# Attention and expert kernel: another issuer for one score row, another fence between bank halves, and TensorE ordered by rules in place of a list

## The chip, the cores and the metric

The kernel runs on one core of one Trainium2 chip. The metric is the device time of one execution in microseconds. Before the change it was 452.55 us, the median of three runs (452.53 to 452.61).

## The reference

Eight sequences of 448 tokens, twelve heads of 64. The first part is attention with capped scores, the second a layer in which each sequence sends its 128 best tokens through a two-layer expert:

```python
scores = cap * np.tanh(scale * (q @ k.T) / cap)      # per batch and head, 448 x 448
attn = np.exp(scores - max); attn /= attn.sum(-1) + 1e-9
x = (attn @ v), heads side by side                   # (8, 448, 768)
s = x[b] @ w_gate                                    # one score per token
top = the 128 tokens of batch b with the highest s
out = x; out[b, top] += sigmoid(s[top]) * (relu(x[b, top] @ w1) @ w2)   # 768 -> 1024 -> 768
```

## The kernel before, in words

**Tiling.** Four heads of one batch make a "double" (class `Double`): 24 doubles, three to a batch. The 448 keys of a double are cut in three chunks of 128 and one of 64. A chunk of 128 is a *unit*: its scores ("Q", `scores_mm`, lines 505 and 515) fill the one four-bank score tile `psS`; ScalarE takes tanh of it into one of four `p` slots (line 970) and exp in place (line 977); then TensorE multiplies it with the values ("V", `values_mm`, line 528, 56 products). The 64-key chunks of two neighbouring doubles share one score tile and one `p` slot and are multiplied one by one. The next Q can start when tanh has read `psS` and a `p` slot is free; the slot is free after its V. From the fifth double on, q and k are split in a high and a low part, and scores come from twelve products of full width (line 505, array shape `WIDTH`). Values run in the shape `TALL`, the rest of the scores and the 64-key values in `QUARTER`.

**Expert work** ("F"). When three doubles of a batch are done, `select_proc` adds their score parts, writes the row of 448 scores to DRAM and reads it back into every partition (`put`, line 632; `get`, line 635), counts ranks on VectorE, picks the rows with a one-hot product (line 711), and gathers them by GpSimd (line 727). `expert_proc` transposes them (line 756), multiplies with w1, applies relu, transposes, multiplies with w2, adds and scatters (line 863). A layer is a `group` (line 783): products of 64 rows in pairs, hi times hi, hi times lo and lo times hi, 72 products for w1 and 96 for w2. In the second half of a group the two row halves change banks; ahead of the first product of that half stands a `drain` of TensorE (line 797).

**Order.** All engines' orders are written by a planner (`Sim`, `Front`) that knows a duration for every task. TensorE's comes from `SCRIPT` (lines 36 to 41): Q or V in a fixed sequence, a number in front of which so many F products are put (`scripted`, line 1101). Where the script is empty, `policy` (line 1061) uses rules: if F is at hand (`backlog`), Q first, F next, V last, until `run_ready` says that four values, or all that are left of the double, can run one after the other; then V first until the double ends. Without F at hand Q and V alternate. Outside the tail only one group may be open, and none is opened once planned F work passes the total less `RESERVE` (50 us). `EARLIER` shifts the priority of single tasks of other engines. GpSimd's queue holds the `put` and `get` of batch 0, a memset for each value tile that lands (line 492), gathers and scatters.

Of the kernel before, what the change touches and what calls it, by code (L numbers as in the profile page):

```python
# [31 lines left out]
THIN_Q, THIN_V, THIN_F = "FVQ", "QFV", "VQF"  # L32
SOON = 1000
FILL = 300

SCRIPT = ("Q Q V V Q V Q V Q V V Q V Q V Q V Q V Q V Q V Q V Q V V Q V Q V Q V Q V Q V Q V Q V Q "
# [5 lines left out]

EARLIER = {('greater', 21): 1, ('hi', 29): -3, ('high', 21): -1, ('high', 23): 3, ('low', 2): -3,
           ('low', 27): -1, ('ranks', 7): -0.4, ('relu', 3): 3, ('relu', 11): 3}

LINE, LATER, FIRST = ("POOL", 1000, 2800, "gpsimd"), ("SP", 700, 900, "sync"), 1


QUARTER, TALL, WIDTH = range(3)
SWITCH, AFTER = 110, 85  # L50
MARGIN = 150
RESERVE = 50000
MOST = 4000
# [5 lines left out]
RUN, SLACK = 4, 300  # L59

SIDE = 6
DRAIN = 100

PS, PG, PH = 1.3, 1.1, 1.2
VISIBLE = {"PE": 230, "DVE": 120, "ACT": 110, "POOL": 150, "SP": 0}
# [51 lines left out]
class Sim:  # L117
# [47 lines left out]
    def finish(self, task, e, start):  # L165
        for x in task.busy:
            self.pend[x].remove(task)
        task.eng, task.start = e, start
        task.slots = []
        for r in task.take:  # L170
            s = r.next()
            r.free.remove(s)
            task.slots.append(s)
        for s, n in zip(task.slots, task.refs):
            s.refs = n
        busy = task.busy[e]
        if e == "PE":
            if task.shape != self.shape:
                busy += AFTER
            self.shape = task.shape  # L180
        end = start + busy
        self.clock[e] = end
        if e == "SP":
            self.dma = max(self.dma, start + 1500) + task.lag
            task.t = max(start + 2600, self.dma)
            end = task.t
        else:
            task.t = end + VISIBLE[e] + task.lag
        for s in task.reads:
            s = s() if callable(s) else s  # L190
            s.t = max(s.t, task.t if e == "SP" else end + 60)
            s.refs -= 1
            if s.refs == 0:
                s.ring.free.append(s)
        task.fn(task)
        if task.waiter is not None:
            w, task.waiter = task.waiter, None
            self.step(w, task)
        self.wake()
# [50 lines left out]
def allocate(tc, K):  # L250
    cp = K.const

    def t(name, shape, dt=F32):
        return cp.tile(shape, dt, name=name)
# [2 lines left out]
    K.cap = t("capc", [P, 1])  # L257
    K.ident = t("ident", [P, P])
    K.fast = t("fast", [1, 1], I32)
    K.sq = t("sq", [1, 1])  # L260
    K.sc = t("sc", [P, 1])
    K.wts = {}
# [518 lines left out]


def group(tc, K, kind, prio, pair, parts, wts, n, width, cost):
    nc = tc.nc
    ops = [(0, wts + "h", i) for i in range(n)] + [(0, wts + "l", i) for i in range(n)]
    ops += [(1, wts + "h", i) for i in range(n)]
    last = len(ops) - 1
    slot, ends, gap = None, [], []
    order = mybir.DependencyInfo(mybir.DependencyClass.NoSync, mybir.DependencyReason.DATA)
    for m in range(2 * len(ops)):  # L790
        turn, at = divmod(m, len(ops))
        part, r, i = ops[at]

        def mm(t, m=m, turn=turn, at=at, part=part, r=r, i=i):
            bank = t.slots[0] if m == 0 else slot
            if m == last + 1:
                gap.append(nc.tensor.drain().ins)
                for end in ends if K.loose else []:
                    tc.add_manual_dep(gap[0], end, order, reason="rows change banks")
            for h in (0, 1) if m != last else (1, 0):  # L800
                g = h ^ turn
                ins = nc.tensor.matmul(bank.obj[:, g, :width],  # L802
                                       lhsT=pair.obj[part][HALF[h], i, :],
                                       rhs=K.wts[r][HALF[h], i, g * width:(g + 1) * width],
                                       start=(m == 0), stop=(m == 2 * last + 1)).ins
                if m == last:
                    ends.append(ins.name)
                elif m == last + 1 and K.loose:
                    tc.add_manual_dep(ins, gap[0].name, order, reason="rows change banks")

        t = yield Task("PE", cost + (DRAIN if m == last + 1 else 0), mm, deps=[parts[i][part]], take=[] if m else [K.banks],
                       refs=[] if m else [2], reads=[pair] if m == 2 * last + 1 else [], prio=prio,
                       kind="mm" if m else "open")
        if m == 0:
            slot = t.slots[0]
            K.open += 1
    K.open -= 1
    return slot, t


def expert_proc(tc, K, b, M, idx, gt, gate, x):
    nc = tc.nc
    sim = K.sim
    S = K.S
    xe = x.slots[0]
    prio = (1, b)
    yield [K.weights["w1"]]
    xs, parts = yield from split_tasks(tc, K, lambda: xe.obj, [x, K.weights["w1"]], K.xs, [],
                                       K.ND, (0, 3 * b + 2), "turnxe")
    xs.refs = 1  # L830
    if not K.tail:
        yield [p for pair in parts.values() for p in pair]
    bank, t = yield from group(tc, K, "w1", (1, 0 if K.tail else b), xs, parts, "w1", K.ND, K.F // 2, 234)
    relus = []
    for g in range(2):
        def relu(t, g=g):
# [5 lines left out]
            else:  # L842
                nc.scalar.activation(out, src, AF.Relu)

        t = sim.add(Task(None, {"ACT": 660, "DVE": 610}, relu, deps=[t], take=[] if g else [K.hs],
                         refs=[] if g else [1], reads=[bank], prio=1, kind="relu"))
    yield [t]
    hp, parts = yield from split_tasks(tc, K, lambda: relus[0].obj, [t], K.hp, [relus[0]],
                                       K.NF, (0, 3 * b + 2), "turnh")
    hp.refs = 1  # L850
    yield [K.weights["w2"]]
    if not K.tail:
        yield [p for pair in parts.values() for p in pair]
    HH = K.DM // 2
    bank, t = yield from group(tc, K, "w2", prio, hp, parts, "w2", K.NF, HH, 177)
    ends = [sim.add(Task("DVE", 534, lambda _, g=g: nc.vector.scalar_tensor_tensor(
        out=xe.obj[:, g * HH:(g + 1) * HH], in0=bank.obj[:, g, :HH], scalar=gt.obj,
        in1=xe.obj[:, g * HH:(g + 1) * HH], op0=ALU.mult, op1=ALU.add), deps=[t, gate],
        reads=[bank, gt], prio=1, kind="combine")) for g in range(2)]
    yield ends  # L860

    def scatter(t):
# [7 lines left out]
               kind="scatter")  # L870


class Front:
# [74 lines left out]
    def score_task(self):  # L948
        K, sim, nc = self.K, self.sim, self.tc.nc
        u = self.u  # L950
        two = self.work[u]
        shape = self.score_shape()
        reads = [x.slots[0] for D, _ in two
                 for x in (D.ready(0, K) if shape == WIDTH else (D.q, D.k))]

        def emit(t):
            for i, (D, s) in enumerate(two):
# [1 line left out]
            self.u += 1  # L959
            self.S_free = None  # L960

        task = Task("PE", 1498 if shape == QUARTER else 1230, emit, shape=shape, reads=reads,
                    kind="scores")
        task.seq = 0
        sim.pend["PE"].append(task)
# [479 lines left out]
```

## Time and profile before

| | |
|---|---|
| median of three runs | 452.55 us |
| profiled execution | 453.71 us, its span 452.0 us |
| busy share of the span | TensorE 95%, weight loads 80%, ScalarE 68%, VectorE 61%, GpSimd 5% |
| granted TensorE clock | 0.995 of full |
| chain that ended last | TensorE 87%, ScalarE 5%, issue 3%, VectorE 2%, DMA 2% |

Busy time is given by engine, in microseconds and as a share of the span; TensorE's matmuls are pipelined and their ends are modelled, so the starts of neighbouring groups say more than the busy time of one. "L528" is line 528 of the kernel. In a timeline a line holds start, duration, engine, source line, operation, tile written and tiles read, shape and count; idle time before it stands in brackets with what ended it.

### The profile page before, as it was taken

How to read it: one execution, taken by the hardware profiler on the slowest of the kernel's cores; microseconds unless marked ns; L12 is line 12 of the kernel's file. 1: busy time of each engine (PE TensorE's matmuls, PEld its weight loads, DVE VectorE, ACT ScalarE, POOL GpSimd, SP SyncE). 2: the span in 40 equal slices, each digit the busy share in tenths (PEclk: the TensorE clock that was granted, in tenths of full speed). 3: DMA queues.
4: the chain of work that ended last, by engine and by line, in shares of the span. 5: the costliest groups of instructions: out<-in, count | busy, mean ns of one | idle time of the engine just before them, and what ended most of it. 6: DMA issues, size and time to landing. Idle time of an engine off the chain costs nothing.

```text
span 452.0 us, 17987 instructions
## 1 busy us (share of the span) xinstructions
PE 431.3 (95%) x8148; PEld 361.1 (80%) x8148; DVE 275.7 (61%) x846; ACT 306.8 (68%) x194; POOL 23.3 (5%) x57
## 2 busy tenths in 40 slices
PE   8889889999999999999999999999999999999993
PEld 6655477779898889898898888889888889879793
DVE  1076778986946588367765766737747665385141
ACT  4979989976697589487778766966689599311000
POOL 2000010000001000000000000000001000000000
PEclk9999999999999999999999999999999999999997
DMA  7958395664073372282372542443172223111001
GB/s 248 374 157 278 108 289 191 186 232 120 3 246 111 81 236 53 74 276 68 90 234 78 155 160 85 138 146 108 38 247 68 77 93 106 35 35 32 39 38 42
DMA packets 34022, 60.76 MB, mean 134 GB/s; under 512 B 11088, under 2 KB 21072, under 8 KB 33936
## 3 DMA queue, kind: packets, MB, share of 16 engines
q1 hardware_dynamic: 32400, 52.73, 36.4%
q0 software_dynamic: 1392, 6.56, 4.7%
q8 instruction: 66, 1.08, 0.9%
q10 hardware_dynamic: 144, 0.23, 0.2%
q14 instruction: 20, 0.16, 0.1%
HBM read 45.33 MB, written 14.17 MB: 132 GB/s over the span
## 4 chain that ended last, share of the span: by engine, by line
PE 87%; ACT 5%; issue 3%; DVE 2%; DMA 2%; POOL 0%; POOLq 0%; DVEq 0%
PE psV L528 30%; PE psT L802 23%; PE psS L505 16%; PE psS L515 8%; PE psB L802 3%; ACT p L970 3%; PE psV L802 2%; ACT p L977 2%; PE psT L756 1%; DMA p<-out,idx 1%; PE psT L1259 1%; ACT plent L970 1%; DVE xn L560 1%; PE psT L711 1%; DMA out<-xe,idx 1%
## 5 line engine op out<-in xcount | busy, mean ns | idle before, releaser
L970 ACT ACTIVATE p<-psS,sc 128x1792 f32<-128x1792 f32 x62 | 108.8, 1755 | 58.6 <-PE psS L505 32.8
L528 PEld LDWEIGHTS psV<-v,p 128*64 128x64 f32 (+1 forms) x3864 | 104.2, 137 | 20.5 <-issue 16.4
L528 PE MATMUL psV<-v,p 128*64 128x65 f32 (+1 forms) x3864 | 111.2, 222 | 4.1 <-issue 2.3
L977 ACT ACTIVATE p<-p,capc 128x1792 f32<-128x1792 f32 x62 | 111.1, 1793 | 1.8
L559 DVE RECIPROCAL rec<-psV 128x7 f32<-128x7 f32 x48 | 9.6, 200 | 71.4 <-PE psV L528 71.3
L505 PE MATMUL psS<-qh,kh 64*128 64x448 f32 x240 | 48.1, 391 | 0.5 <-ACT plent L970 0.4
L970 ACT ACTIVATE plent<-psS,sc 128x1792 f32<-128x1792 f32 x21 | 36.8, 1753 | 16.8 <-PE psS L505 12.0
L528 PEld LDWEIGHTS psV<-v,plent 128*64 128x64 f32 (+1 forms) x1288 | 35.0, 137 | 7.7 <-issue 6.9
L977 ACT ACTIVATE plent<-plent,capc 128x1792 f32<-128x1792 f32 x21 | 37.6, 1793 | 0.6
L528 PE MATMUL psV<-v,plent 128*64 128x65 f32 (+1 forms) x1288 | 37.5, 222 | 0.4 <-DVE xt L565 0.4
L515 PE MATMUL psS<-q,k 64*64 64x448 f32 x312 | 34.4, 549 | 2.5 <-ACT p L970 1.6
L594 DVE CUSTOM_DVE_ANT_0 jk<-xn,wg 128x256 bf16<-128x256 f32 x72 | 30.3, 421 | 1.4
L560 DVE TENSOR_TENSOR xn<-psV,rec 128x384 f32<-128x384 f32 x48 | 26.8, 557 | 1.9 <-DVE rec L559 0.3
L505 PEld LDWEIGHTS psS<-qh,kh 64*128 64x128 f32 x240 | 23.3, 184 | 4.0 <-ACT plent L970 0.5
L664 DVE TENSOR_SCALAR_CACHE_REDUCE jk<-row,score 128x512 bf16<-128x512 f32 (+1 forms) x32 | 23.7, 741 | 0.8
L472 DVE CAST kh<-k 128x896 fp32r<-128x896 f32 x20 | 12.8, 638 | 16.0 <-PE psS L505 15.7
L505 PE MATMUL psS<-qh,kl 64*128 64x448 f32 x120 | 22.4, 363 | 0.0
L505 PE MATMUL psS<-qh,klent 64*128 64x448 f32 x120 | 22.4, 362 | 0.0
L505 PE MATMUL psS<-qlent,kh 64*128 64x448 f32 x120 | 22.4, 362 | 0.0
L505 PE MATMUL psS<-ql,kh 64*128 64x448 f32 x120 | 22.3, 362 | 0.0
L515 PEld LDWEIGHTS psS<-q,k 64*64 64x64 f32 x312 | 10.2, 132 | 14.3 <-issue 10.2
L802 PE MATMUL psT<-w1h,xh 64*128 64x512 f32 x144 | 20.5, 407 | 0.7
(163 smaller groups left out, 619.8 us busy)
## 6 DMA issues: line engine op xcount, KB each, us to landing
v<-in_v SPq DMA_DIRECT2D x23, 455.0 KB, 4.5
q<-in_q SPq DMA_DIRECT2D x22, 448.0 KB, 4.5
k<-in_k SPq DMA_DIRECT2D x22, 448.0 KB, 5.2
out<-xn SPq DMA_DIRECT2D x24, 384.0 KB, 3.6
stage<-in_moe_w SPq DMA_DIRECT2D x4, 512.0 KB, 8.0
stage<-in_moe_w SPq DMA_DIRECT2D x5, 384.0 KB, 4.0
row<-line SPq DMA_DIRECT2D x7, 256.0 KB, 3.3
out<-xt SPq DMA_DIRECT2D x48, 32.0 KB, 3.4
```

What stands on the lines that cost most here:

```text
L472: nc.vector.tensor_copy(t.slots[0].obj, self.at(nm))
L505: tc.nc.tensor.matmul(banks[2 * r + j][:, :K.S], lhsT=a[HALF[j], r, c * P:(c + 1) * P], rhs=b[HALF[j], r, :], start=(n == 0), stop=(n == 2))
L515: tc.nc.tensor.matmul(banks[n][HALF[half], :K.S], lhsT=k[HALF[j], r, at:at + HD], rhs=q[HALF[j], r, :], start=True, stop=True)
L528: tc.nc.tensor.matmul(D.acc.obj[HALF[g], r, i * WIDE:(i + 1) * WIDE], lhsT=p[rows, h, n * HD:(n + 1) * HD], rhs=v[rows, u, :], start=(c == ...
L559: nc.vector.reciprocal(rec, blocks[:, :, K.D])
L560: nc.vector.tensor_tensor(slots[0].obj.rearrange("p c (r j d) -> p r j c d", r=2, j=2)[:, r], blocks[:, :2 * full, :K.D].rearrange("p (j c ...
L594: nc.vector.tensor_tensor_reduce(out=K.jk[:, :x.shape[1]], in0=x, in1=g, scale=1.0, scalar=0.0, op0=ALU.mult, op1=ALU.add, accum_out=part[ ...
L664: nc.vector.tensor_scalar(K.jk[:m], row[:m], score[:m, c:c + 1], None, op0=ALU.is_gt, op1=ALU.add, accum_out=rk.obj[:m, 0, c:c + 1])
L711: nc.tensor.matmul(t.slots[0].obj[:, h, :4], lhsT=sel.obj[half, c, :], rhs=vals[half, :, c], start=(c == 0), stop=(c == NCH - 1))
L802: ins = nc.tensor.matmul(bank.obj[:, g, :width], lhsT=pair.obj[part][HALF[h], i, :], rhs=K.wts[r][HALF[h], i, g * width:(g + 1) * width], ...
L970: nc.scalar.activation(slot.obj, K.S4[:, :, :K.S], AF.Tanh, scale=K.sc)
L977: nc.scalar.activation(slot.obj, slot.obj, AF.Exp, scale=K.cap)
```

## The change

The script and the list of shifted priorities are emptied, so that TensorE follows the rules. The planner's durations are changed: what a change of array shape costs depends on the pair of shapes, a group's products and the `QUARTER` scores get other lengths, the drain's length goes. Batch 0's `put` and `get` are issued by ScalarE's queue. In a group, ahead of the second half, a memset of one element on GpSimd waits for the last two products of the first half, and the first product of the second half waits for that memset; the planner may put other TensorE work between. The general path (not run here, `K.loose`) keeps the drain.

```diff
-SCRIPT = ("Q Q V V Q V Q V Q V V Q V Q V Q V Q V Q V Q V Q V V Q V Q V Q V Q V Q V Q V Q V Q "
-          "V12 Q3 V Q Q V V V V Q14 Q8 V Q17 V V Q V10 Q13 Q17 V Q V6 Q V V Q V Q11 V Q V V Q7 Q13 Q7 "
...
-EARLIER = {('greater', 21): 1, ('hi', 29): -3, ('high', 21): -1, ('high', 23): 3, ('low', 2): -3,
-           ('low', 27): -1, ('ranks', 7): -0.4, ('relu', 3): 3, ('relu', 11): 3}
-
-LINE, LATER, FIRST = ("POOL", 1000, 2800, "gpsimd"), ("SP", 700, 900, "sync"), 1
+SCRIPT = ""
+EARLIER = {}
+
+LINE, LATER, FIRST = ("ACT", 420, 3200, "scalar"), ("SP", 700, 900, "sync"), 1
...
-SWITCH, AFTER = 110, 85
+SWITCH = 40
+AFTER = {(TALL, WIDTH): 104, (TALL, QUARTER): 102, (QUARTER, WIDTH): 90, (QUARTER, TALL): 70,
+         (WIDTH, TALL): 100, (WIDTH, QUARTER): 60}
...
-DRAIN = 100
...
-                busy += AFTER
+                busy += AFTER.get((self.shape, task.shape), 0)
...
+    K.fence = t("fence", [1, 1])
...
-    order = mybir.DependencyInfo(mybir.DependencyClass.NoSync, mybir.DependencyReason.DATA)
+    order = mybir.DependencyInfo(mybir.DependencyClass.NoSync if K.loose else
+                                 mybir.DependencyClass.Sync, mybir.DependencyReason.DATA)
+
+    def fence(t):
+        gap.append(nc.gpsimd.memset(K.fence, 0.0).ins)
+        for end in ends:
+            tc.add_manual_dep(gap[0], end, order, reason="rows change banks")
+
+    passed = []
...
-            if m == last + 1:
+            if m == last + 1 and K.loose:
                 gap.append(nc.tensor.drain().ins)
-                for end in ends if K.loose else []:
+                for end in ends:
                     tc.add_manual_dep(gap[0], end, order, reason="rows change banks")
...
-                elif m == last + 1 and K.loose:
+                elif m == last + 1:
                     tc.add_manual_dep(ins, gap[0].name, order, reason="rows change banks")
 
-        t = yield Task("PE", cost + (DRAIN if m == last + 1 else 0), mm, deps=[parts[i][part]], take=[] if m else [K.banks],
-                       refs=[] if m else [2], reads=[pair] if m == 2 * last + 1 else [], prio=prio,
-                       kind="mm" if m else "open")
+        t = Task("PE", cost, mm, deps=[parts[i][part]] + (passed if m == last + 1 else []), take=[] if m else [K.banks],
+                 refs=[] if m else [2], reads=[pair] if m == 2 * last + 1 else [], prio=prio,
+                 kind="mm" if m else "open")
+        yield t
+        if m == last and not K.loose:
+            passed.append(sim.add(Task("POOL", 100, fence, deps=[t], prio=0, kind="fence")))
...
-    bank, t = yield from group(tc, K, "w1", (1, 0 if K.tail else b), xs, parts, "w1", K.ND, K.F // 2, 234)
+    bank, t = yield from group(tc, K, "w1", (1, 0 if K.tail else b), xs, parts, "w1", K.ND, K.F // 2, 231)
...
-    bank, t = yield from group(tc, K, "w2", prio, hp, parts, "w2", K.NF, HH, 177)
+    bank, t = yield from group(tc, K, "w2", prio, hp, parts, "w2", K.NF, HH, 173)
...
-        task = Task("PE", 1498 if shape == QUARTER else 1230, emit, shape=shape, reads=reads,
+        task = Task("PE", 1560 if shape == QUARTER else 1230, emit, shape=shape, reads=reads,
```

## Rows read from the trace of the kernel before

**Rows 1.** Busy time by stretch: length, then each engine's busy us (instructions), clock, DMA.
```profile
0.00:90.00 90.00, 80.94 (x1672) 56.38 (x1672) 54.78 (x154) 76.89 (x47) 6.13 (x25) 1.00 0.70 228
90.00:391.50 301.50, 298.98 (x5935) 260.01 (x5930) 194.77 (x611) 225.27 (x139) 13.27 (x28) 1.00 0.40 125
391.50:452.00 60.50, 51.37 (x548) 44.66 (x548) 26.11 (x83) 4.61 (x9) 3.86 (x4) 0.96 0.14 41
```

**Rows 2.** The same, of line 802 (expert products): TensorE and its weight loads.
```profile
90.00:391.50 301.50, 100.47 (x876) 79.16 (x876) 1.00 0.40 125
391.50:452.00 60.50, 49.53 (x468) 41.57 (x468) 0.96 0.14 41
```

**Rows 3.** The same, of line 528 (values).
```profile
90.00:391.50 301.50, 116.21 (x4095) 109.77 (x4090) 1.00 0.40 125
```

**Rows 4.** Timeline of TensorE around the first expert group's middle.
```profile
91.61 1.56 PE L802 MATMUL psT<-w1l,xh 64*128 64x512 f32 x12
93.01 0.37 PE L505 MATMUL psS<-qh,kh 64*128 64x448 f32 x2
...
94.23 0.84 PE L802 MATMUL psT<-w1h,xl 64*128 64x512 f32 x6
95.00 1.85 PE L528 MATMUL psV<-v,p 128*64 128x65 f32 x56
96.78 0.47 PE L505 MATMUL psS<-qh,kh 64*128 64x448 f32 x2
...
98.11 0.86 PE L802 MATMUL psT<-w1h,xl 64*128 64x512 f32 x6
99.06 1.43 PE L802 MATMUL psT<-w1h,xh 64*128 64x512 f32 x10
100.32 0.37 PE L505 MATMUL psS<-qh,kh 64*128 64x448 f32 x2
```

**Rows 5.** Timeline of TensorE, the last run of values.
```profile
385.34 1.85 PE L528 MATMUL psV<-v,p 128*64 128x65 f32 x56
387.02 1.80 PE L528 MATMUL psV<-v,plent 128*64 128x65 f32 x56
388.66 2.78 PE L528 MATMUL psV<-v,p 128*64 128x65 f32 x112
```

**Rows 6.** Instructions of line 797: engine, operation, count, duration ns min/median/max, starts.
```profile
L797 PEldq DRAIN  x16: 457/2212/2725, 96.8 to 437.8; - x16
```

**Rows 7.** Timeline of ScalarE where scores and values alternate.
```profile
62.78 1.75 ACT L970 ACTIVATE p<-psS,sc 128x1792 f32<-128x1792 f32 x1 [1.22 <-PE psS L505]
64.56 1.79 ACT L977 ACTIVATE p<-p,capc 128x1792 f32<-128x1792 f32 x1
...
81.15 1.74 ACT L970 ACTIVATE plent<-psS,sc 128x1792 f32<-128x1792 f32 x1
```

**Rows 8.** Timeline of GpSimd, batch 0's `get`.
```profile
62.10 0.59 POOL L635 DMA_DIRECT2D row<-line  x1 [3.30 <-DMA line<-score]
```

**Rows 9.** Instructions of line 492, GpSimd's memsets of value tiles.
```profile
L492 POOL MEMSET v<- x23: 122/124/129, 8.6 to 366.9; 128x14 f32 x23
```

**Rows 10.** DMA issues: tiles, queue, count, size, median us from issue to landing.
```profile
row<-line SPq DMA_DIRECT2D x7, 256.0 KB, 3.3
...
row<-line POOLq DMA_DIRECT2D x1, 256.0 KB, 6.8
```

**Rows 11.** Instructions of line 1244, the one transfer that ScalarE issues.
```profile
L1244 ACTq DMA_DIRECT2D q<-in_q x1: 392/392/392, 0.8 to 0.8; - x1
```

**Rows 12.** Timeline of VectorE and GpSimd in the tail.
```profile
409.74 0.69 DVE L539 CAST hlent<-psA 128x512 fp32r<-128x512 f32 x1 [1.73 <-ACT hlent L539]
...
411.67 0.86 DVE L701 TENSOR_SCALAR sel<-iota,rk 128x128 fp32r<-128x128 f32 x4
...
414.63 0.16 DVE L739 RECIPROCAL gt<-gt 128x1 f32<-128x1 f32 x1
...
414.96 0.95 POOL L727 DMA_INDIRECT p<-out,idx  x1 [36.32 <-DVE gt L739]
```

More of the change, by code (lines that the diff above doesn't have):

```diff
@@ L34 @@
 FILL = 300
-SCRIPT = ("Q Q V V Q V Q V Q V V Q V Q V Q V Q V Q V Q V Q V Q V V Q V Q V Q V Q V Q V Q V Q V Q "
[5 rows of a table removed]
-EARLIER = {('greater', 21): 1, ('hi', 29): -3, ('high', 21): -1, ('high', 23): 3, ('low', 2): -3,
-           ('low', 27): -1, ('ranks', 7): -0.4, ('relu', 3): 3, ('relu', 11): 3}
-LINE, LATER, FIRST = ("POOL", 1000, 2800, "gpsimd"), ("SP", 700, 900, "sync"), 1
+SCRIPT = ""
+EARLIER = {}
+LINE, LATER, FIRST = ("ACT", 420, 3200, "scalar"), ("SP", 700, 900, "sync"), 1
 QUARTER, TALL, WIDTH = range(3)
-SWITCH, AFTER = 110, 85
+SWITCH = 40
+AFTER = {(TALL, WIDTH): 104, (TALL, QUARTER): 102, (QUARTER, WIDTH): 90, (QUARTER, TALL): 70,
+         (WIDTH, TALL): 100, (WIDTH, QUARTER): 60}
 MARGIN = 150
@@ L783, in group @@
 def group(tc, K, kind, prio, pair, parts, wts, n, width, cost):
-    nc = tc.nc
+    nc, sim = tc.nc, K.sim
     ops = [(0, wts + "h", i) for i in range(n)] + [(0, wts + "l", i) for i in range(n)]
```

5 rows, old and new, of the table SCRIPT are left out of this document.

## The prediction

> **What bounds the kernel now.** I read the busy time by stretch first, because the whole span's 95% for TensorE hides three stages [rows 1]. Up to 90 us ScalarE is busy for 76.9 of 90 us and TensorE for 80.9, with starting up in both; no expert product runs yet, so nothing can fill what TensorE waits. From 90 to 391.5 us TensorE is busy for 299.0 of 301.5 us while ScalarE does 225: TensorE alone sets the pace, and only its work, its changes of shape and its idle time count. From 391.5 us attention is over, and the last batch's chain (ranks, gather, two layers, scatter) runs beside what is left of the expert work. That work is split [rows 2]: 876 of its products lie before 391.5 us and 468 behind.
>
> Next the timeline of TensorE for what things cost from start to start. Twelve score products between expert products take 94.23 - 93.01 = 1.22 us, behind values 98.11 - 96.78 = 1.33 [rows 4]. A unit of values takes 95.00 to 96.78 = 1.78 us alone, and 388.66 - 387.02 = 1.64 inside a run [rows 4, 5]. The three pairs ahead of it start 0.77 us before it, where at 0.233 a pair (93.01 - 91.61 over six pairs) they should need 0.70. So one run of values between full-width work costs 0.14 + 0.11 + 0.07 = 0.32 us over its products. From the first run at 95.00 to the last one, whose units are shown [rows 4, 5], I count 47 runs in that timeline after 90 us.
>
> **The change, part by part.**
>
> *Drains out.* There are 16 [rows 6]. Around the first, three pairs and the drain take 99.06 - 98.11 = 0.95 us in place of 0.70, and the five pairs behind it 100.32 - 99.06 = 1.26 in place of 1.17: 0.34 us each. Their own duration of 2.2 us is mostly waiting for products that run anyway. Ten lie before 391.5 us: -3.4 us. Of the six behind it two are on the last batch's chain.
>
> *Fences in.* The memset itself is like those of the value tiles, 124 ns [rows 9]. GpSimd starts 0.17 us after the VectorE result that it waits for (414.63 + 0.16 to 414.96) [rows 12]; no row shows GpSimd releasing TensorE's products, and I take the same there. So the trip lasts some 0.17 + 0.12 + 0.17 = 0.47 us, an estimate from these rows; bare, it costs more than the drain. In attention the planner can put a Q there (nothing, the same shape) or values (one more run, 0.32). Half and half over ten: +1.6 us, between 0 and 10 x 0.47 = 4.7. In the tail the second layer of the last batch has nothing to put between: +0.47 for -0.34; the first layer has other products: -0.34. Together -0.2. Ahead of a fence in GpSimd's queue can stand a memset that waits for a value tile, or a gather of 0.95 us [rows 12].
>
> A rule speaks against the fence. The Trainium skill ("SBUF — State Buffer", Who interferes with whom) has GpSimd share a port pair with VectorE under an exclusive lock, so that one blocks fully while the other runs an instruction in a two-port mode. The rows show no stretch: 23 memsets lie within 122 to 129 ns [rows 9], though a wait ahead of the start would not show there. By the rule each fence could wait for one VectorE cast, some 0.7 us [rows 12], which belongs to the fence rival below.
>
> *Order by rules.* This is the big term, and no row shows the rules at work; I work out their cycle. With expert work at hand they put expert products between scores until a whole double's values can run. A double is 3.5 units. ScalarE needs 3.5 x (1.75 + 1.79) = 12.4 us for them [rows 7]. All four `p` slots are then full, so the next scores come only behind the run: 3.5 x 1.64 + 1.33 = 7.1 us, of which the last exp covers 1.8. ScalarE idles 5.3 us and the cycle is 17.7 us. TensorE spends 3.5 x (1.22 + 1.64) + 0.32 = 10.3 of it, which leaves 7.4 us for expert work. Expert work before 391.5 us is 100.5 us busy, with modelled ends [rows 2]; I take 95. That feeds 95 / 7.4 = 12.8 doubles. Values in that stretch are 4095 / 224 products = 18.3 doubles [rows 3], so 5.5 run without expert work, scores and values in turn. Where the kernel does that now, five units take 81.15 - 62.78 = 18.37 us, 3.67 each [rows 7]: 12.8 us a double, of which TensorE needs 10.0 + 3.5 x 0.32 = 11.1. It idles 1.7 us a double, 9.5 in all, against 2.5 now [rows 1]. Runs of values become 12.8 + 5.5 x 3.5 = 32, 15 fewer: -4.8 us. Net +2.2, between -4.8 - 2.5 (never idle) and +29 (18.3 doubles x 1.7 with no run saved).
>
> *Expert work moved.* Rules that are greedy finish a first layer once it is open. 876 products are five batches of 168 and 36; the other 36 of that group, 18 pairs x 0.233 = 4.2 us, would come out of the tail into the stretch that TensorE bounds. The tail hangs on the last batch's chain and gives little of it back; I take +2.1, from 0 to 4.2.
>
> *Row of batch 0 through ScalarE.* The transfer back took 6.8 us from GpSimd's queue and takes 3.3 from SP's [rows 10], and GpSimd sat 3.30 us for the first landing [rows 8]. But the planner gives each transfer 420 + 3200 where it gave 1000 + 2800, so what follows on VectorE is put in nearly the same place: 0.2 us earlier each. ScalarE issues twice, 0.39 us each by its one transfer [rows 11], at most GpSimd's 0.59 [rows 8]; behind them wait tanh and exp. 0.8 us against an earlier start of the experts: 0, from -1 to +1.5. The Trainium skill ("DMA: Bandwidth & Descriptors", Latency and other measured facts) gives 0.6 us to the first byte from ScalarE's queue and 1 us from GpSimd's. By it the change of queue brings 0.4 us a transfer; the rows of this case differ by 3.5, so the measurement decides, and either is earlier than the planned place uses.
>
> *Shifted priorities out.* In the tail the one-hot of the last batch starts at 411.67, behind a cast and subtractions of batch 6's work from 409.74 on [rows 12]. Another order may free up to 1.9 us of that or put a second such block ahead. 0, between -1.9 and +1.9.
>
> **Sum.** -3.4 + 1.6 + 2.2 + 2.1 - 0.2 = +2.3 us. The profiled execution took 453.71 us (span 452.0, 1.7 around it), which gives 456.0; the median of the runs lies 1.16 us below the profiled execution, so 454.9, rounded to 455.0 us.
>
> **Rivals.**
>
> 1. *The rules cost no idle time.* If fences and the lag of expert work break the long runs up, ScalarE gets its scores earlier, thin stretches shrink, and TensorE stays at 2.5 us idle. Then -3.4 - 4.8 + 1.6 + 2.1 - 0.2 = -4.7, 447.9 us; with the moved work also at 0, 445.8. For it: the 76 us that ScalarE has free in the middle stretch [rows 1]. Against it: four slots, all full at a run. It decides below about 5 us idle there.
> 2. *Fences stand bare or behind others.* Ten at 0.47 + 0.7 us instead of 0.16 add 10.1 us: 465. For it: GpSimd's queue runs in order, and the memsets of value tiles wait for transfers. Against it: the queue is nearly empty, 13 us busy in 301 [rows 1].
> 3. *The parts cancel.* Idle time of 7 us in the middle and no work moved: 452.5. For it: every term is of the size of the others.
> 4. *The tail decides.* The chain of the last batch loses or wins a block of 1.9 us; inside the other cases.
>
> **Chances.** Forecast 0.44, rival 1 0.34, rival 2 0.12, rival 3 0.10. The likeliest case alone is 453.6 to 460. Eight times in ten: 445.5 to 464.0, which leaves out the lower end of rival 1, most of rival 2's upper half and the far end of the idle term. Within 0.2% of 452.55, some 0.9 us, is what this measurement can't tell from no change: 0.10; faster 0.36 (rival 1 and a little of rival 3), slower 0.54.
>
> **What would show it.** No drain rows; first products of second halves waiting for GpSimd by 0.5 us or less, or scores between. In TensorE's timeline some 32 runs of values after 90 us, more of 3 and 4 units. TensorE idle of 7 to 12 us between 90 us and the end of attention, put down to ScalarE, and ScalarE waiting for scores some 5 us at a time. The end of attention near 394 us and 432 products of line 802 behind it. Waits of a microsecond on GpSimd's memset would speak for rival 2; idle time of 3 us and an end of attention before 388 us for rival 1. A tail that is not 60 us would make the prediction wrong for a reason that I put at nothing.

## The result and the profile after

The changed kernel takes 459.19 us, the median of four runs (455.90 to 461.12), beside 452.58 for the kernel before in the same session: 1.0139 times its time [1.0098, 1.0180]. The forecast was 455.0 with a range of 445.5 to 464.0, so the sign and the range held, and the size (+2.4 forecast, +6.6 measured) was little over a third of what came. The four runs differ with their mean granted clock: 455.90 at 0.998, 458.81 at 0.991, 459.57 at 0.992, 461.12 at 0.989. (Where a median and its ratio do not agree below, e3 and e6, a disturbed run or two is in the median and not in the ratio.) The profiled execution is the last one; its span is 459.4 us, 7.4 more than before.

The first view is again busy time by stretch, cut at the new end of attention, 392.5 us, with one stretch more in the middle (columns as in [rows 1]).

```profile
0.00:90.00 90.00, 79.64 (x1668) 56.53 (x1672) 53.43 (x152) 74.81 (x46) 5.28 (x23) 1.00 0.69 225
90.00:392.50 302.50, 293.71 (x5856) 256.19 (x5848) 195.06 (x611) 225.48 (x139) 14.73 (x37) 0.99 0.39 123
392.50:459.40 66.90, 59.07 (x640) 52.22 (x632) 26.48 (x84) 4.61 (x10) 6.14 (x12) 0.97 0.16 49
159.00:165.80 6.80, 6.20 (x86) 5.32 (x88) 4.56 (x15) 5.04 (x4) 0.13 (x1) 0.50 0.57 212
```

Against [rows 1]: in the middle TensorE idles 302.50 - 293.71 = 8.8 us where it idled 2.5, that is 6.3 more; up to 90 us 10.4 where it was 9.1, 1.3 more; in the tail 7.8 where it was 9.1, 1.3 less. Its busy time grew by 432.42 - 431.28 = 1.1, and that hides two things: for 6.8 us the granted clock was 0.50, 1.2 GHz in place of 2.4, with 6.2 us of products in it, which cost some 3 us (half of it by the clock, 43% by the spacing of the score pairs, last section); the rest of the work became 1.5 to 2 us shorter. 6.3 + 1.3 - 1.3 + 1.1 = 7.4, the whole difference of the spans. So the loss has two places: idle time in the middle, and a slow clock.

The same for the expert products, which answers [rows 2].

```profile
90.00:392.50 302.50, 88.31 (x792) 72.65 (x792) 0.99 0.39 123
392.50:459.40 66.90, 56.65 (x552) 49.03 (x552) 0.97 0.16 49
```

84 products have moved out of attention into the tail (552 behind its end, 468 before); the forecast had 36 moving in. Next the waits of TensorE in the middle (us in total, times, longest; "issue" is time in which the engine waited for nothing that the profile shows).

```profile
PE psT L750 <- DMA xe<-out,idx: 3.2, 1, 3.2
PE psS L499 <- issue: 1.6, 1, 1.6
PE psV L522 <- DVE both L715: 1.3, 2, 0.8
PE psV L522 <- issue: 1.1, 2, 0.8
PE psV L522 <- ACT p L982: 0.7, 1, 0.7
```

Single waits stand here, each for another reason, and only 0.7 us is put down to ScalarE. The longest is shown by the timeline of SyncE, GpSimd and TensorE around it, and by the landing time of the gather.

```profile
151.40 1.72 POOL L721 DMA_INDIRECT xe<-out,idx  x1 [3.25 <-DVE gt L733]
151.57 1.14 SPq L441 DMA_DIRECT2D q<-in_q  x1
...
155.09 0.33 SPq L441 DMA_DIRECT2D v<-in_v  x1
...
155.85 0.37 PE L499 MATMUL psS<-ql,kh 64*128 64x448 f32 x2
156.06 0.37 PE L499 MATMUL psS<-qh,kl 64*128 64x448 f32 x2
159.60 0.91 PE L750 MATMUL psT<-ident,xe 64*128 64x64 f32 x12 [3.18 <-DMA xe<-out,idx]
...
161.50 0.61 PE L499 MATMUL psS<-qh,kh 64*128 64x448 f32 x2
161.88 0.60 PE L499 MATMUL psS<-ql,kh 64*128 64x448 f32 x2
```

Batch 1's gather is issued at 151.40. From 151.57 to 155.09 SyncE issues the q and k loads of the next two doubles and one v load beside it, and the transposes that read the gathered rows stand next in TensorE's order at 156.4, 5.0 us behind its issue. Behind the wait the score pairs start 0.37 us apart, where they stood 0.21 apart just ahead of it: the clock has fallen. Landing times of that batch's gather, changed kernel and then the kernel before:

```profile
DMA to landing us min/median/max: 3.4/5.8/8.1
```

```profile
DMA to landing us min/median/max: 3.9/3.9/3.9
```

The 8.1 is the gather, the 3.4 the scatter ahead of it. Before, one v load was issued 3.0 us behind this gather, the transposes started 4.2 us behind its issue, and TensorE did not wait for it (timelines of GpSimd, SyncE and TensorE):

```profile
141.33 0.98 POOL L727 DMA_INDIRECT xe<-out,idx  x1 [4.01 <-DVE gt L723]
144.37 0.33 SPq L447 DMA_DIRECT2D v<-in_v  x1
145.55 0.53 PE L756 MATMUL psT<-ident,xe 64*128 64x64 f32 x12
```

### The profile page after: what moved, and what is told of

It reads as the page before. It is cut to its first block, busy times and chain, and to the rows that moved or that the text cites. A ratio compares the mean times of both kernels' runs of the same rounds, so it can differ in the third digit from the quotient of the medians.

```text
span 459.4 us, 18004 instructions
## 1 busy us (share of the span) xinstructions
PE 432.4 (94%) x8148; PEld 364.9 (79%) x8148; DVE 275.0 (60%) x846; ACT 304.9 (66%) x194; POOL 26.2 (6%) x71
## 4 chain that ended last, share of the span: by engine, by line
PE 81%; DMA 6%; DVE 4%; ACT 4%; issue 3%; SPq 0%; POOL 0%; POOLq 0%; DVEq 0%
PE psV L522 28%; PE psT L804 23%; PE psS L499 16%; PE psS L509 6%; PE psA L804 4%; ACT p L975 2%; PE psB L804 2%; DMA k<-in_k 2%; DMA xe<-out,idx 2%; DMA row<-line 2%; ACT p L982 1%; PE psT L750 1%; DVE klent L472 1%; DMA out<-p,idx 1%; DVE jk L658 1%
## 5 line engine op out<-in xcount | busy, mean ns | idle before, releaser
L522 PE MATMUL psV<-v,p 128*64 128x65 f32 (+1 forms) x3864 | 113.2, 223 | 6.4 <-issue 2.4
L499 PE MATMUL psS<-qh,kh 64*128 64x448 f32 x240 | 49.2, 403 | 1.4 <-DVE vals L677 0.8
L975 ACT ACTIVATE plent<-psS,sc 128x1792 f32<-128x1792 f32 x21 | 36.8, 1752 | 10.1 <-PE psS L499 8.9
L522 PE MATMUL psV<-v,plent 128*64 128x65 f32 (+1 forms) x1288 | 38.5, 226 | 0.8 <-issue 0.8
L509 PE MATMUL psS<-q,k 64*64 64x448 f32 x312 | 35.5, 549 | 2.4 <-ACT p L975 1.1
L804 PE MATMUL psT<-w1l,xh 64*128 64x512 f32 x168 | 23.6, 393 | 0.0
L804 PE MATMUL psT<-w1h,xh 64*128 64x512 f32 x168 | 23.3, 406 | 0.1
L804 PE MATMUL psT<-w1h,xl 64*128 64x512 f32 x168 | 22.2, 392 | 0.0
## 6 DMA issues: line engine op xcount, KB each, us to landing
v<-in_v SPq DMA_DIRECT2D x23, 455.0 KB, 4.0
```

Source lines behind the costliest of these rows:

```text
L499: tc.nc.tensor.matmul(banks[2 * r + j][:, :K.S], lhsT=a[HALF[j], r, c * P:(c + 1) * P], rhs=b[HALF[j], r, :], start=(n == 0), stop=(n == 2))
L509: tc.nc.tensor.matmul(banks[n][HALF[half], :K.S], lhsT=k[HALF[j], r, at:at + HD], rhs=q[HALF[j], r, :], start=True, stop=True)
L522: tc.nc.tensor.matmul(D.acc.obj[HALF[g], r, i * WIDE:(i + 1) * WIDE], lhsT=p[rows, h, n * HD:(n + 1) * HD], rhs=v[rows, u, :], start=(c == ...
L804: ins = nc.tensor.matmul(bank.obj[:, g, :width], lhsT=pair.obj[part][HALF[h], i, :], rhs=K.wts[r][HALF[h], i, g * width:(g + 1) * width], ...
L975: nc.scalar.activation(slot.obj, K.S4[:, :, :K.S], AF.Tanh, scale=K.sc)
```

## The experiments

Each was run in five rounds beside the kernel before; each expectation names its own theories. "Idle" is the stretch from 90 us to the end of attention less TensorE's busy time in it; "slow" is time at granted clock 0.50 in the profiled execution, the last microseconds of the span left out; "behind" is expert products after attention. For the kernel before the three are 2.5, 0 and 468.

| | median us | ratio, 95% interval | idle | slow | behind |
|---|---|---|---|---|---|
| the change | 459.19 | 1.0139 [1.0098, 1.0180] | 8.8 | 6.8 | 552 |
| e1 | 457.96 | 1.0102 [1.0072, 1.0132] | 7.3 | 3.4 | 552 |
| e2 | 454.59 | 1.0039 [1.0022, 1.0056] | 4.2 | 0 | 468 |
| e3 | 460.73 | 1.0179 [1.0143, 1.0214] | 6.3 | 0 | 552 |
| e4 | 453.82 | 1.0027 [1.0004, 1.0050] | 3.2 | 0 | 462 |
| e5 | 458.31 | 1.0111 [1.0092, 1.0131] | 7.7 | 3.4 | 504 |
| e6 | 461.11 | 1.0131 [1.0085, 1.0176] | 9.9 | 6.8 | 600 |
| e7 | 474.19 | 1.0459 [1.0436, 1.0482] | 20.2 | 10.2 | 600 |
| e8 | 469.73 | 1.0365 [1.0345, 1.0385] | 14.2 | 6.8 | 600 |
| e9 | 452.51 | 0.9998 [0.9985, 1.0011] | 4.4 | 0 | 600 |
| e10 | 460.83 | 1.0180 [1.0159, 1.0200] | 8.7 | 6.8 | 636 |
| e11 | 462.95 | 1.0235 [1.0216, 1.0255] | 11.6 | 10.2 | 468 |
| e12 | 457.28 | 1.0100 [1.0075, 1.0125] | 5.5 | 0 | 600 |

**e1, the loads held behind the gather.** The changed kernel, every order kept; the first of the five loads waits for batch 1's gather.

```diff
+            if self.d == 12 and nm == "q":
+                tc.add_manual_dep(ins, K.second, ...)   # K.second: batch 1's gather
```

> The changed kernel, every engine in the same order; only SyncE's load of q for the thirteenth double waits until the second batch's gather has landed, so that the five loads that ran beside that gather start behind it. Theory 1 (the loss is TensorE's idle time and its clock: the gather landed in 8.1 us instead of 4.2, TensorE waited 3.2 us for it and then ran 6.8 us at half clock): the gather lands in some 4.2 us, the wait falls below 0.5 us, the granted clock stays full until the end, the time is 452.5 to 455 us and the executions agree within 1 us instead of 5. Theory 2 (the rules push 84 more expert products behind the end of attention and the tail's chain is what is longer): 458 to 460 us, the wait was incidental. Against theory 1 also: the held loads land 4 us later and something else waits up to 4 us for them.

The wait shrank from 3.2 to 0.8 us and the slow stretch behind it went. The gather did not land in the 4.2 us that was expected without the loads, but in 5.9 (the largest of the three):

```profile
DMA to landing us min/median/max: 3.6/4.8/5.9
```

Another slow stretch came 100 us later, behind a stall that the change has too (1.58 us at 260.6, without a fall of the clock):

```profile
255.36 0.36 PE L502 MATMUL psS<-qh,kl 64*128 64x448 f32 x1
257.84 0.47 PE L502 MATMUL psS<-qh,kl 64*128 64x448 f32 x1 [2.12 <-issue]
```

```profile
259.10:262.50 3.40, 3.40 (x24) 3.33 (x22) 3.37 (x12) 2.79 (x2) 0.00 (x0) 0.50 0.16 33
```

The second is busy time in the stretch behind it, at granted clock 0.50. The stall is inside a unit of scores, between two products of one pair, and nothing that the profile shows ends it. The intervals of e1 and the change overlap: to shorten the wait for the gather does not by itself bring the time back, and theory 1's 452.5 to 455 us did not come.

**e2, bare fences in the old order.** The kernel before, all orders kept; in place of each drain a memset on GpSimd that the second half waits for.

```diff
-                gap.append(nc.tensor.drain().ins)
+                gap.append((nc.tensor.drain() if K.loose else nc.gpsimd.memset(K.fence, 0.0)).ins)
```

> The kernel before, script and orders of TensorE, VectorE, ScalarE and SyncE unchanged; in place of each of the 16 drains stands the fence through GpSimd, with nothing put between. By the prediction a bare fence is 0.47 us and a drain 0.34: 16 x 0.13 = +2.1, 454.7 us. By the two bare fences in the trace of the changed kernel (0.43 and 0.46 us ahead of the second half and 0.10 to 0.12 behind) it is 0.55: +3.4, 456.0 us. If fences stand behind others in GpSimd's queue (rival 2 of the prediction): 458 us or more. If TensorE loses nothing to them: 447 us.

454.59, 1.9 us above the kernel before in its session (452.65). Its waits name the fence:

```profile
PE psT L804 <- POOL fence L799: 3.1, 10, 0.7
...
PE psB L804 <- POOL fence L799: 0.5, 2, 0.3
```

Some 0.3 us of idle time a fence, 0.7 at worst. Over 16 places the exchange of a drain for a bare fence loses 1.9 / 16 = 0.12 us each.

**e3, the row back on GpSimd's queue.** The changed kernel with the old `LINE`; only GpSimd's and ScalarE's orders differ.

```diff
-LINE, LATER, FIRST = ("ACT", 420, 3200, "scalar"), ...
+LINE, LATER, FIRST = ("POOL", 1000, 2800, "gpsimd"), ...
```

> The changed kernel with the first batch's row issued by GpSimd again; TensorE, VectorE and SyncE keep the same order. The prediction put the change of queue at 0, from -1 to +1.5. Theory 1: the same as the changed kernel, 455.9 to 461.1 us with a spread of several us, since the second batch's gather is untouched. If ScalarE's issues cost something in the stretch that ScalarE bounds, it is 1 to 1.5 us faster; if the earlier row was worth something, 1 us slower.

460.73 beside 459.19, with intervals that overlap: the queue of one row is worth nothing that this measurement tells. The profiled execution, 455.76 us, is the quickest of its runs; there batch 1's gather, with the same five loads issued from 0.6 us behind it on, landed in 5.7 us and kept TensorE 0.4, and no slow stretch came, with the order of TensorE unchanged. So the wait and the slow clock vary from run to run. Gather and stretch:

```profile
DMA to landing us min/median/max: 3.4/4.5/5.7
```

```profile
90.00:386.80 296.80, 290.45 (x5844) 253.63 (x5842) 194.13 (x610) 224.48 (x138) 13.14 (x37) 1.00 0.40 125
```

This execution shows what the order costs without them: 3.1 us over the kernel before (452.65), with 6.3 us idle in the middle, of which the stall "issue" inside the scores is 1.6 again and the rest waits of 0.8 us and less. The change's own run at the clock 0.998 took nearly the same, 455.90.

**e4, the rules alone.** The kernel before with an empty script and no shifted priorities.

```diff
-SCRIPT = ("Q Q V V Q V Q V Q V V Q V Q V ...
+SCRIPT = ""
-EARLIER = {...}
+EARLIER = {}
```

> The kernel before with the script and the shifted priorities emptied and nothing else: drains, old durations, row through GpSimd. The prediction's terms of order and moved work give 452.6 + 2.2 + 2.1 = 456.9 us, with some 32 runs of values after 90 us. Theory 1: what it costs is seen as TensorE's idle time (or its clock), and the number of expert products behind the end of attention doesn't matter; time = 452.6 + the idle time added. Theory 2: it has more than 600 products of the expert behind the end of attention, and 458 us or more without added idle time.

453.82, 1.2 us above the kernel before. Runs of values after 90 us fell from 47 to 39 (the changed kernel has 46), and idle time in the middle rose by 0.7:

```profile
90.00:393.00 303.00, 299.77 (x5970) 260.30 (x5966) 196.08 (x618) 222.76 (x136) 15.66 (x28) 1.00 0.40 125
```

**e5, the drains back in the changed kernel.** The rules, the corrected durations and ScalarE's row, with the drains (and `DRAIN = 100`) of before.

```diff
-            passed.append(sim.add(Task("POOL", 100, fence, ...)))
+        t = yield Task("PE", cost + (DRAIN if m == last + 1 else 0), mm, ...)
```

> The changed kernel with drains (and their planned 100 ns) in place of the fences; rules, new durations and the row through ScalarE stay, and the planner orders anew. The rules alone took 453.8 us with 2.8 us of TensorE idle between 90 us and the end of attention, the changed kernel 459.2 with 6.3 to 8.8. Theory D (the new durations let the planner put work where the chip isn't ready): the idle time stays at 6 us or more, 457 us or more. Theory F (the fences and what is put between them do it): 453 to 455 us, idle below 4.

458.31: without one fence it is as slow as the change. Against e4 only the durations and the row's queue differ, and e3 prices the queue at nothing in the order of the change; so the corrected durations bring some 4 us (4.5 by the medians, 3.8 by the ratios to the kernel before), through the order that they make.

**e6, the old durations in the changed kernel.**

```diff
-SWITCH = 40
-AFTER = {(TALL, WIDTH): 104, ...}
+SWITCH, AFTER = 110, 85
```

(also 234, 177 and 1498 in place of 231, 173 and 1560)

> The changed kernel with the durations of before (110 and 85 for a change of shape, 234, 177, 1498); rules, fences and the row through ScalarE stay. Theory D: idle time between 90 us and the end of attention falls to 3 us or less, no drains are left, so 453.8 - 16 x 0.34 + two bare fences = 449 to 451 us. Theory F: 456 us or more, as in the changed kernel.

461.11. So it is not that the new durations are bad in themselves: with fences the old ones do no better. Batch 1's gather kept TensorE 4.5 us, and the clock was at 0.50 for 6.8 us from within that wait on.

**e7 and e8, fences and script together.** e7 is the kernel before with the planned fences; e8 is the changed kernel with the old `SCRIPT` and `EARLIER`.

```diff
+            passed.append(sim.add(Task("POOL", 100, fence, deps=[t], prio=0, kind="fence")))
```

```diff
-SCRIPT = ""
+SCRIPT = ("Q Q V V Q V Q V Q V V Q V Q V ...
```

> The kernel before with fences as tasks of the planner in place of the drains, and nothing else: script, shifted priorities, old durations, row through GpSimd. Bare fences in the old order took 454.6 us. With work between them, theory D: 16 drains less and few bare fences, 448 to 450.5 us. Theory F: 454 us or more, since the expert products that wait for a fence leave their places in the script.

> The changed kernel with the script and the shifted priorities of before put back; fences, new durations and the row through ScalarE stay. Theory O (the order by rules is what loses): 448 to 451 us. Theory D or F: 455 us or more, with idle time of TensorE above 5 us between 90 us and the end of attention in spite of the script.

474.19 and 469.73, the worst of all. As I read it, the list counts expert products between scores and values, a group that must stop for a fence does not have them at hand, and their places in the list pass; what the trace shows is 600 products left behind attention. The middle of e7 has 20.2 us without a product:

```profile
90.00:401.70 311.70, 291.50 (x5794) 251.08 (x5790) 193.12 (x608) 223.18 (x137) 14.48 (x36) 0.98 0.38 117
```

**e9, a later planned gather.** The changed kernel with one number altered.

```diff
-                       reads=[idx], lag=2600, prio=1, kind="gather"))
+                       reads=[idx], lag=10600 if b == 1 else 2600, prio=1, kind="gather"))
```

> The changed kernel with one number of the planner altered: the landing of batch 1's gather is planned at 10.6 us behind its issue in place of 2.6, so the transposes that need it are placed later in TensorE's order. Theory 1 (TensorE waits where the plan is tighter than the chip; a wait in the middle is paid in full, and half of the slow-clock stretch behind it once more): no wait above 1 us near 156 us, no half clock behind it, idle time from 90 us to the last run of values below 7 us where the changed kernel has 8.8, time 453 to 456.5, runs within 2 us of one another. Theory 2 (more expert products behind the end of attention are the cost, 552 against 468): time 458 to 460 whatever that wait does. A new order may put a wait in another place; then theory 1 expects last product = work of 429 to 434 us + idle time + half of the slow-clock time all the same.

452.51 us (451.41 to 454.02, 12 runs): the whole loss is gone, and the ratio to the kernel before is 0.9998. Stretches, then the timeline, then the gather's landing:

```profile
90.00:378.70 288.70, 284.27 (x5804) 247.79 (x5793) 195.30 (x608) 224.83 (x136) 14.19 (x35) 1.00 0.42 129
378.70:450.70 72.00, 63.29 (x696) 56.92 (x688) 27.97 (x91) 4.48 (x10) 6.43 (x13) 0.97 0.15 46
sum 450.70, PE 427.20 PEld 361.19 DVE 276.45 ACT 303.79 POOL 26.01; mean PE 142.40 PEld 120.40 DVE 92.15 ACT 101.26 POOL 8.67
```

```profile
156.35 0.37 PE L499 MATMUL psS<-qh,kl 64*128 64x448 f32 x2
158.56 0.47 PE L499 MATMUL psS<-qh,kh 64*128 64x448 f32 x2 [1.85 <-ACT p L975]
...
164.05 0.53 PE L750 MATMUL psT<-ident,xe 64*128 64x64 f32 x12
```

```profile
DMA to landing us min/median/max: 8.4/8.4/8.4
```

The gather lands just as late; the transposes stand 7 us later, and nobody waits for it. A wait of 1.85 us for ScalarE came in its place, where none above 1 us was expected, and no slow stretch follows. Against the change the span is 8.7 us shorter: 4.4 less idle in the middle, 5.2 less busy time (some 3 of it the slow clock's), 0.9 more in the tail. But the one number makes a new order of TensorE from 160 us on, without the stall near 260 us too, and its span is 3.3 us shorter even than that of e3's profiled execution (454.0), which had no slow clock in the middle and hardly a wait for the gather. So e9 shows what the edit is worth, not what the wait alone is.

**e10, room everywhere.** The gathers at 10.6 and 4.6 us, and the planner's margin on a dependency at 400 in place of 150.

```diff
-MARGIN = 150
+MARGIN = 400
```

> The changed kernel with more room in the plan: batch 1's gather planned at 10.6 us, the other gathers at 4.6 us in place of 2.6, and the planner's general margin on a dependency 400 in place of 150. Theory 1: idle time in the middle falls below 5 us, no fall of the clock before the last products, time 449 to 454. Theory 2: the time follows the number of expert products behind the end of attention, at 552 some 458 to 460. A third theory (the fences themselves cost, however the plan stands): 456 or more with idle time still at 7 to 9 us.

460.83: this went against the theory. The new order avoids the old wait and makes others, the longest of them for a q load:

```profile
PE psV L522 <- DMA q<-in_q: 3.0, 1, 3.0
PE psS L499 <- issue: 2.1, 2, 1.8
```

Room in the plan is not by itself what helps. And e10 holds e9's number: to plan for the one wait is not enough when the order that follows has others.

**e11, one wait put into the kernel before.** Its orders kept; twenty small instructions on GpSimd, the second of which reads the picked rows' numbers, stand ahead of batch 1's gather.

```diff
+            if b == 1 and not K.loose:
+                nc.gpsimd.memset(K.late, 0.0)
+                nc.gpsimd.tensor_copy(K.late[:M, :1], idx.obj[:M, :1])
+                for _ in range(18):
+                    nc.gpsimd.tensor_scalar(K.late[:M], K.late[:M], 0.0, None, op0=ALU.mult)
```

> The kernel before with the same order on TensorE, VectorE, ScalarE and SyncE; on GpSimd twenty small instructions that depend on the picked rows stand ahead of batch 1's gather, so it is issued some 2.5 to 4.5 us later (one injected wait of that length on TensorE near 145.5 us, where the transposes of that batch stand). Theory 1: the wait is paid in full, 455 to 457 without a fall of the clock, and 456.5 to 459 where the granted clock falls to half behind the wait as it did behind 156 us in the changed kernel. Rival (free time elsewhere absorbs it, since expert work can run later): within 1 us of the kernel before, 452.5 to 453.5.

The delay came out longer than meant, 8.79 us in 18 of them, so the expected times do not apply. Timeline of GpSimd and TensorE, then the stretch at the slow clock:

```profile
140.25 8.79 POOL L732 TENSOR_SCALAR late<-late 128x80 f32<-128x80 f32 x18
144.09 0.37 PE L506 MATMUL psS<-qh,klent 64*128 64x448 f32 x2
153.53 0.90 PE L762 MATMUL psT<-ident,xe 64*128 64x64 f32 x12 [9.07 <-DMA xe<-out,idx]
```

```profile
146.90:157.10 10.20, 3.57 (x62) 3.48 (x64) 2.59 (x9) 1.19 (x1) 3.00 (x7) 0.50 0.20 57
```

The median rose by 462.95 - 452.81 = 10.1 us, the span of the profiled execution by 461.2 - 452.0 = 9.2: 9.1 more idle time in the middle, which is the wait in full; 1.5 more busy time, of which the 3.57 us at the slow clock are some 1.5 to 1.8 (43% to a half); less 1.1 up to 90 us and 0.3 in the tail. Nothing later took any of it back, with 468 expert products still to come. The rival that free time elsewhere absorbs a wait falls.

**e12, drains again in the order of e9.** All orders kept; the second halves drain and wait for no memset.

```diff
+            if m == last + 1 and not K.loose:
+                nc.tensor.drain()
...
-                elif m == last + 1:
+                elif m == last + 1 and K.loose:
```

> The kernel with the later planned gather (452.51 us), every engine's order kept as it is, but in front of each second half of a group TensorE drains again, and no product waits for GpSimd's memset any more (the memsets themselves stay). Theory 1 (a drain costs 0.34 us at every place where it stands and a fence with work planned between costs next to nothing): 16 x 0.34 = 5.4 us more, 457 to 458.5, idle time about the same and the work 434 us where it was 429. Rival (the fences cost as much as the drains, and the shorter work comes from the order alone): within 1 us of 452.5.

457.28, where the expectation had 457 to 458.5: the fences of the change are worth 457.28 - 452.51 = 4.8 us in the order of e9, 0.3 us a place.

```profile
90.00:380.80 290.80, 285.33 (x5796) 247.78 (x5788) 194.79 (x607) 224.83 (x136) 13.85 (x35) 1.00 0.41 128
```

In the profiled execution, 456.01 us, 2.3 us more of it is busy time and 1.0 more idle in the middle; the split between the two is not settled by one execution.

No version beats both kernels: e9 equals the kernel before.

## Why the prediction was right in sign and a third in size

**What bounds the kernel** held. From 90 us to the last product TensorE is packed, so idle time in the middle is paid in full (e11), and it was the term to watch. The forecast put all that idle time down to ScalarE; ScalarE ended 0.7 us of it.

**Drains and fences**, -3.4 + 1.6 - 0.2 = -2.0. The bare fence was forecast 0.13 dearer than the drain, 2.1 us over 16, and e2 measured 1.9. The half that was to be covered was nearly all covered. In the changed kernel only two of the 16 fences kept TensorE, both in the tail where nothing stands between:

```profile
398.21 1.56 PE L804 MATMUL psA<-w1l,xh 64*128 64x512 f32 x12
399.61 1.55 PE L804 MATMUL psA<-w1h,xl 64*128 64x512 f32 x12
401.44 1.66 PE L804 MATMUL psA<-w1h,xh 64*128 64x512 f32 x12 [0.28 <-POOL fence L787]
402.94 1.33 PE L804 MATMUL psA<-w1l,xh 64*128 64x512 f32 x10
...
448.07 1.68 PE L804 MATMUL psT<-w2h,hlent 64*128 64x384 f32 x16 [0.28 <-POOL fence L787]
```

Twelve products that need 399.61 - 398.21 = 1.40 us take 1.83 up to the fence, 0.43 more, and the twelve behind it 402.94 - 401.44 = 1.50, 0.10 more: 0.53, where 0.47 was estimated (from parts that add up to 0.46). So the term was mis-sized by the share that is covered: -4.8 (e12, in the order of e9) in place of -2.0.

The rule on the shared port came true after all. The Trainium skill ("SBUF — State Buffer", Who interferes with whom) has one of VectorE and GpSimd blocked fully while the other holds the pair. The rows of before showed none of it [rows 9]; the changed kernel does. First the fence memsets (ns min, median, max), then one of them in the timeline with VectorE:

```profile
L787 POOL MEMSET fence<- x16: 89/89/705, 99.6 to 447.9; 1x1 f32 x16
```

```profile
170.92 0.70 POOL L787 MEMSET fence<- 1x1 f32 x1 [7.26 <-PE psT L804]
170.97 0.62 DVE L466 CAST qh<-q 128x896 fp32r<-128x896 f32 x1
```

An 89 ns memset lasts 705 and ends at 171.62, with VectorE's cast at 171.59. The trace agrees with the rule in place and in size, the 0.7 us that the prediction named. Two more of the 16 were stretched, to 518 and 247 ns, and each ended 0.03 us behind such a cast; the other 13 took 89 or 90 ns, five of them while VectorE was busy. None of the three kept TensorE; at 170.92 it had 2.5 us of values to run (78 products from 170.69 on). Rival 2, all fences bare and blocked, did not come.

**Order by rules**, +2.2. Alone it cost +1.2 (e4), by other parts than forecast: 39 runs of values in place of 32, idle time in the middle 3.2 in place of 9.5. In the changed kernel the 15 runs that were to be saved are not: it has 46, one of them of four units. The cycle of whole doubles with all four slots full was worked out from no row, and it is the exception.

**Expert work moved**, +2.1. Wrong in sign and in worth: 84 products moved out, and no run shows a price for it. With 600 products behind attention e9 takes 452.51, with 468 the kernel before 452.81. A tail of 66.9 us in place of 60 was named as a sign of a wrong prediction; it was one, of this step.

**The row through ScalarE**, 0, held (e3). ScalarE's two issues took 0.34 and 0.33 us, and no activation waited for them; the 1.28 us ahead of the tanh is put down to TensorE:

```profile
57.01 0.34 ACTq L626 DMA_DIRECT2D line<-score  x1
58.45 1.76 ACT L975 ACTIVATE p<-psS,sc 128x1792 f32<-128x1792 f32 x1 [1.28 <-PE psS L509]
...
60.30 0.33 ACTq L629 DMA_DIRECT2D row<-line  x1
```

The 2 KB that go out landed in 2.4 us from ScalarE's queue and in 3.2 from GpSimd's (e3; 3.7 in the kernel before). The Trainium skill ("DMA: Bandwidth & Descriptors", Latency and other measured facts) has 0.4 us between such queues to the first byte (0.6 and 1); the measured 0.8 has its sign and twice its size.

**Shifted priorities out**, 0. They were emptied only together with the script (e4) or put back with it (e8), so no run prices them alone.

**The step that failed** is one that the prediction did not take. It priced the edits one by one and gave the corrected durations no price at all. What they and the fences do is make a new plan, and that plan put batch 1's transposes 5.0 us behind the issue of a gather that landed in 8.1. In the profiled execution the wait (3.2 us), a stall inside the scores (1.6) and the slow clock (some 3) add up to 7.8 us, where the span grew by 7.4. But they are not all of the loss: without that wait and without a slow clock in the middle the same order took 455.8 (e3) and 455.9 us, some 3 above the kernel before, in the stall and in small waits that the old order did not have. That leaves at most some 5 us, different from run to run, for the wait and the slow clock. e9 takes the whole loss away, by another order. The order of before had been free of such a wait, and its clock did not fall before the last products; the forecast took both for given. The sum came near because its terms erred on both sides: -2.0 for -4.8, +2.2 for +1.2, +2.1 for 0, and nothing for some +10 (6.3 + 1.3 us more idle time and some 3 us of slow clock, of which e4's +1.2 holds a part). That the sign came right is luck in good part. Of the rivals, 1 fell with the idle time, 3 with the slow clock, and the tail of rival 4 gave 1.3 us of idle time back. (Rival 3's terms come near its 452.5 only if its 7 us are added to the 2.5 of before; taken as they stand they give 450.3.)

What stays open: which of the corrected durations makes the order worse (e5 against e4; with the old ones and fences it is no better, e6), how the loss splits between the wait, the slow clock and the small stalls in a run that is not the profiled one, and what ends the stalls that the profile puts down to "issue".

## What to carry to other kernels

When a planner writes the order, every edit of a duration or a task is an edit of the whole order. Look first in the new trace for the one or two waits of over a microsecond on the engine that bounds, and ask which landing or stall they hang on: here one transfer's planned landing (2.6 us planned, 8.1 measured), set to 10.6, made an order that is 6.7 us faster, while the edits as such were worth 1 to 5 us each. That order has to be measured again: with the same number and more slack elsewhere (e10) the time was 460.83. And price an edit in its own order only, by a pair like e9 and e12, where one thing differs and no instruction moves.

## What the runs showed of the hardware that was not expected

**The clock falls in the middle of the kernel.** In the kernel before it stayed at full speed until 447 us. It fell inside waits of 3.18 us (the change), 4.49 (e6) and 9.07 (e11), and behind waits of 2.12 (e1) and 1.51 (e5); behind waits of 1.58 us (the change, at 260.6) and 1.85 (e9) it did not. It came back after 3.4, 6.8 or 10.2 us. Score pairs were 0.37 us apart instead of 0.21, so the products of such a stretch lose somewhat less than half of it. The Trainium skill ("TensorE: Matmul & The Clock Gate", Terms) puts the penalty at the throttled time times one minus the clock's share, here half; the spacing gives 1 - 0.21 / 0.37 = 43%.

**One gather's landing varies from 3.9 to 9.3 us.** Batch 1's gather landed in 3.9 us in the kernel before and in 8.1 to 9.3 where five loads of some 450 KB were issued from 0.2 us ahead of it to 0.2 us behind it on (the change, e6, e9, e10, e12). The loads do not explain it alone: with the same five from 0.6 us behind it on it took 5.7 (e3), and with none of them 5.9 (e1). GpSimd's issue of it took 0.97 us in e3 and 0.98 in the kernel before, 1.3 to 1.9 in the other six. What each part adds is not shown.
